# Fused RWKV-5 and tanh-shrink kernel: first four w_in pieces on SyncE's queue, own terms of units one to three as TensorE products, and another written order

## The chip, the core and the metric

One core of a Trainium2 chip runs the whole program. The metric is the device time of one execution in microseconds. Three runs of the kernel before took 582.51, 583.96 and 585.50 us; their median is 583.96 us. All times below are of that chip, in microseconds from the start of the profiled span unless said otherwise.

## What is computed

The first block is an RWKV-5 recurrence for 4 batches, 8 heads, 768 steps and heads of 48. The second is a dense layer with h - tanh(h) between two products. The output of the first, laid out as 3072 tokens of 384, is the input of the second.

```python
for t in range(S):
    kt, vt, rt = (k[:, :, t], v[:, :, t], r[:, :, t])
    cur = np.einsum('bhd,bhe->bhde', u[None] * kt, vt)
    y[:, :, t] = np.einsum('bhd,bhde->bhe', rt, state + cur)
    state = w[None, :, :, None] * state + np.einsum('bhd,bhe->bhde', kt, vt)
...
h = x @ w_in                 # 3072 x 384 by 384 x 2048
g = h - np.tanh(h)
out = g @ w_out              # 3072 x 2048 by 2048 x 384
```

The term of step t with itself, r_t * u * k_t summed over the head's 48 numbers, is what the kernel calls the own term. The two weight matrices come as float64 and are turned into float32 on the chip.

## The kernel before, in words

**Units.** The recurrence is cut into 24 units of 64 steps and two batches. A unit loads r, k and v in two halves each (96 KB a half, 192 bytes a packet), turns r and k over on TensorE into PSUM (L654, L806, L808), scales them by powers of w on VectorE and ScalarE (`scale_r`, `scale_k`, `copy_k`), and makes the 64 x 64 score matrices of its heads (`levels`, L730, all small products recorded at L606). VectorE copies what lies before the diagonal into the tile `at` (L830). The diagonal is the own term. `outputs` (L741) then multiplies `at` with v, `to_xt` and `to_rest` (L774, L779, ScalarE, recorded at L765) carry the result into the dense layer's input `xt`, and `to_state` and `keep` (L755, L789) go on with the state.

**Own terms.** A unit below `OWN` makes them as a product: ScalarE scales the turned k by w*u in four instructions (`own_k`, L706 to L709), TensorE makes 16 small products (`own_levels`, L711; each is two records in the trace), and VectorE copies the diagonal in one instruction (L821). A unit from `OWN` on does three VectorE instructions (r*k, times u, a sum over the head; L694, L824, L698) and eight small ScalarE instructions (`diagonal`, L702). `OWN` is 1, so unit 0 alone makes products.

**Dense layer.** Tile (j, f) is 256 tokens by 256 of the 2048 columns: 12 tiles j, of two units each, by 8 steps of f, 96 in all. It is: `h` in two halves of six TensorE records (L217), five ScalarE instructions (Arctan, Tanh, Tanh, Square, Relu: s, th, tg, sq, small), three on VectorE (g, m, cp; L242 to L246), and the product with w_out, either plain (`o`, L254) or with seven products for eight (`products`, L307), for which GpSimd adds parts of g (L290 to L294). PSUM holds two h tiles: `h` of the next tile but one waits for g of this one.

**Weights.** w_in and w_out come in 16 pieces (`Weights`, L134 to L191). A w_in piece is four loads: two main ones of 288 KB and two rests of 96 KB. The main ones go through SyncE's queue, the rests through GpSimd's (L589). A piece is then converted in seven steps on VectorE and ScalarE (L185 to L191). The pieces of w_in are numbers 0, 1, 4, 5, 8, 9, 12 and 13, the others are w_out.

**Loads.** All loads of a unit from unit 2 on are issued by SyncE; of units 0 and 1 ScalarE's queue issues the second halves (L647). From the second unit pair on, a part of the dense layer's input is moved across partitions by six loads per pair from GpSimd's queue, from the tile `rest` to `xt` (L786).

**Order.** `lay_out` (L540) makes 2400 tasks with an engine each. `Plan.written` (L364) emits them in the order of the string `ORDER`: each two characters are a task's number. Each engine executes its own instructions in that order and waits for what each needs. Numbers past the tasks are fill products on TensorE with the identity, whose result nobody reads (`fills`, L532, recorded at L534), and the place where the flag of w's range is read. The costs and data figures given to `add` take no part in what is emitted.

Of the kernel before, what the change touches and what calls it, by code (L numbers as in the profile page):

```python
# [42 lines left out]

DIGITS = "0123456789ABCDEFGHIJKLMNOPQRSTUVWXYZabcdefghijklmnopqrstuvwxyz+_"
ORDER = (
    "00010J2f2g2h2i2j2k2l2m2n0HbWbX02030K040605bWbWbW2o2q3534363231332r2t0I2s07370A0FbWbX080B0C2u2x2y38392v092w3U0D3C"
    "3B3V3W2p3A3G0U2z0L3R0M2+3S3T3D2_0N3F3H0V3Y0O3I0T3u3E3J0PbWbX3L3K3b0QbX3c300S3M3v3w3a0R3r3e3N3s3t3d0w3O3f3P3X3Z3g"
    "8D3Q3h3i3k0W0G3_4O3j0X8E0d430Y4P4Q3l4L0Z44404M4N453m8F0a3y463+0b3n413o0c423p3x3z15470ebYbYbY484p0u0E4Z8I4o4q0f8P"
    "4a0g494l0h4b4S4A4V4c0i4U4R4T4B3q4W0j8Q4m4n4C4X5I4v4Y4J5J5K4D8H4F0k4dbZ4e4K0l4I8L8R5F4G4f8G4H5G5H4z8SbZ4w134s8K8J"
    "4g5i8T8M8U4u4E4h8N4+8W4i4x8O8X8V4r4t4_8d4y4j5f505T0m525j5k510n5g5h5U8e0o8Y5L5V0p8p535M5N5W0q6C548g5P6D6E5X0r5O0t"  # L50
    "550s5Q698q5R5m565t6A6B8Z4k5S5A578h5lba5n595u8f5D5Y5p8i5B5v8j5C8a5Z5E5w6d8k8l5q6c6e8c5x5a6Z8m6N8b5o5b0v8n5r6a6b58"
    "145c6J8o6F5s5d6G6H8s6O775y8t6P6Q915z8r5e746R6n5+6o8u8w6I5_6j6K926L7678606p6g8x9D6M6373758v61666q688y6S6f6h676r64"
    "7W8z656T7X7Y9562946U937U98967T7V7H6i6V1D7I6k9E7J970xJ+996W9RJ_K06l6m796X7K0yJx9S6Y9H9F6s9I9J8+JyJz6t9T7A7B7h9G8_"
    "6u9K7L7D9A7C6vKP7EKM9d7F7G7a7i6w129e7j7Z7b906z6x7k9L6_KLKN9B6+7d9VKOKQ726y9WK9707M7l719C9X7N0z9M7cKA9U7O9f9YKu0+"
    "9Z7eKvKw7P9a9rKr7fK29i0_9N7Q1L7g7R9OKsKt9j16K1K3KZ9P177m9Q109h9g9b7n1811197o9l9k9s7p1ELF1F1TKBA17qKRL3LGLH9tKa7t"
    "9c1G7vKb7y9m9v7wA29w1A7u1H7x9z9n9xK61B9uLI9o9pLl9yA41CA5AFA3A81e1hKC1MLJLK1fAG1N9q1WKSKTA6KW1U1VAR1OA91g9+1PASAH"
    "1QAI9_A7L4AUAAA0AKAJAVANABKcAM1RALAfKD1SAgAT1I1xADLmLnAWAOACLoAYAjLpLqAZAiArAh7SAmAkAsAXL5AEAaB31iAv1jAtMAAP1J1k"
    "AnAwB41KAlAuAz1pAQAxAyM9MBB6AoBFA+B7LT1lBGBAB51mBTBH1nBIBJAb1XB81YMfB91oAcMgMh1ZBM2G2H1aBBBU2FBCBKBfAeBNBV1bBYBg"
    "Ad1cBXBWApBiBaBL1dAqBh1qBk2324KxA_1r26Bb251sKyKzBOB01t2E1yB1BjBt1z1u1+BuBm1_1vBZC3B2Bv1wByBDBcBw2P20BxC4BlB+BzBn"
    "BE27C5B_BP28Bo2921CH2AC82BBQC9C0C7CIC6BSBRCBBdCJCACM22BeCLCK2XCNCOCTKd2CBp2D2QBqCP2RCUBs2SCC2TChLzL+N4CWBrCXCiN3"  # L60
    "N52UCVCY2IC1CZCaCj2VCtCm2WCkC2CQCbClCDCnCpCoCE2JCq2KCuCF2LCGCcCRCw2MCvCyD52NCz2OCxD62YCS2ZD8C+D92aCdDCD7CeDACf2b"
    "DBDKCg2cDL7rC_DZD0DMDNDDDODa2dDP2eCrDbDRDcDe89CsDQDEDSD1DdDFDgDGDoDT85DUDp86DHEEDqDVDrDsEFDtDvDf87D2Du88EH81ETD3"
    "LUEUDhD4EGDwDIDiEVDxEJDjDJEIEKELDXDkEX8ADlEYEiEWDyEZEaDWEj8BDz8CD+ExEMEyENEbEmDYElEcE+82EkDmEpEOEn83E_FNEqEzF0Eo"
    "FOF3LVErDnFP84FQD_F2FSEd7sE1EeFRE0E2F1E3EPE4ERFTEQE5E6E7ESFVFUFcF4FdF5EsEgFgEtFeEfFfEhFhFjFrFiE8FWE9FsEBEAFkFXFl"
    "EvFuECFt7zFYFwG4FvEDFyFZG5F6FzEuEwG8F7FxGWFmG6F+G9FnF8G7GAGBFAGCF9FBFCGXF_FDGDG0GlGZFEFFFoGYFGGbFaFKGa7+Fb7_FHFp"
    "GeGE80GmFMGdFLFqGFGnFIGpG+GGGoG1GqFJGcG_GfG2GtH2GgGsH1GrG3H5GhH0GiGHGJH3GKGIGLH4GMHDGNGOGQHEGPGTH6HfK5HFH7HGGuGj"
    "HHGvHIHgHKGwHLH8HuHhK4GxHiH9HJHvGVHjGSHMHkHAGkHmHlK8HxI7HNHwKVHnHzHOGyH+HPHyGzHBK7HCI0KUH_KEHoI8HpHqKYIMHrIAGUI9"
    "KFGRLPICINI1IDIBI2HQIOIEI3IPI4KXIQIoIRIFIpK+IGIUKGIsHSISHTHRITIqL6IVJ1IHHUL7HVK_HsHWHXKHHYJ2KIHtIrKJJ5IvItKeHcIu"
    "IwHeJ4JGL1HdJ3IWJ6I5J8IIJ7LuIXHZIYJHKfHaIxHbKgL2JKIJJJJIJVJ9KhLOL0KKI6L_JLLWJWJNJAKiIKJOJMKnKjLXKpLQILLvIyJPJXIZ"
    "IzJZJYKoJaL8JBIbJbIcJCIaIdI+IeJcKlI_LMIfJQMCIgKqMDMEIhJ0JDIlKmIiJEJRJdInKkJFIkL9ImMjPJMNIjMiMkLRJSPKLSLAPNMOPMMJ"  # L70
    "JeJTPLPQPOJfPPMtPYJgLBPRJhPZMPLCPSLwPnNZPTPaLDMIPdPUPbPoPVPcPfLYPqPrJUPpPuPeJiN6PsNaNbPtPvQ0JkLLLNPgPwQ1PhLxPiQF"
    "Q2Q3LZMoQ4QGJlLyLaQHQ7Q5MuQIJjLEQKJmLbJnPWMKMpJoJpLcQUJqQJLkQ6QVLiQMPjJuPxPXLdQXJrM0JvLsM2QNPkNzMQQ8N7N8JsQjM1Lj"
    "Q9LrLtPyQLPlPzQWQAQOMRPmLgM3QYP+QPQZQbQaJwMvMFM4MLQQMGMHLfQkQRN+N_M5MMQBQyQCQlLeQmLhQcQoQzMmQpQdMlMnM6P_NcQnMwQD"
    "QqQeMqQ+JtRMM7R1QfM8Q_QgQrMxMSQsR2QEMsR0RNQtR3NjQSQuROQvRPRRRbRQRSRTQTR4RcR5MrR6QhReRfRUNiRdRqRVRgRiRhQiMTNHRrRW"
    "NIRXQwRjRtNdNeRYRuNARsQxR7RxN9NBRvR8RkS3NCRwRlS4RmSIS5S8SJS6O0S9NDS7R9SLSARBRCRARDREMURFRGRHRZNJMVRLNgNESBOURaMW"
    "NfNhNKRoMeMXO1O2RyMcMZRzSKSXRnSMR+SNMySPSOR_SQS0RpSROWSYSCOXOYOTOVSSSmSaSDSbSZSnMdSeScMaNnMbMzS_SoRKOrMYSdSTOsOt"
    "T0SpRISqSESrSFStS1SsSuT2SvS2NoSfSGSgTPT3ShT1T6SiT4TQOBSjNFSUTeTRT7TSO6NLSHTTM+SwTUSxTXTfM_SyTWSVT5TVT8TtTYTiN0Np"
    "OhSWThTuTlT9NkSkN1TxOvTgOuOwTjSlTvSzNqTZTwRJU6TAT+TBNGTaU7TbTmO7S+U9TkNMTyTnTzTCT_U8UATETDUDO4TFU0ULNmU1UMToTGOd"
    "THUaTIUNTMUPTpUOUbUBTqUSUQN2TcUdNNUCOCO3O5UpURUTTJUqTKUUTOODU2NOP3U3NlTNTdNPUETrOcNQUFOETsUGUcUHU4UeNYUfNTUhNrU5"
    "UINRNXOZNSUrUVNsOiUsUtUWV2O9UgUXOFNVUJUiNUO+UuUjUKNtUkUwV3NWOAUYV5UxUvO_UZV6UyV4V9NuUzP4U+OjUnNvU_TLVSUlOkOaObUm"  # L80
    "V7VTV8VAOlVBVhVUVCVXViOxVDVYVEOyOzUoVjVWV0VVVlVZVmV1VaVnVbVwVkVpVoVxVqVFO8V+VrVzVHVsW1NwVGVcVIVyNxW9VdV_NyVeW0VJ"
    "W2OGVKVLVfVMVNOHVgOeW3OIP5W4WAP0W5OfVtVuW6WBWEVQVvWDVOP6W7WCWFWGW8OJWHWOWIOgWJWPWMWSOKWdWQOOOLP7OROMOSOmWROPOQWe"
    "OnWKONWVWLP2OoWhVPWgWsWfP1OpWtWkWTWUWWX5WiWuWlX6OqWXWwWYWNWvWZWxWbWaX8W+WjWzP8WyWmXVX9WnP9W_PAXCX0WoXWPBX1X2WpWc"
    "X7VRXAWqXBXDXZXEWrXXXaXFXkXbXdXGXYX3XHXcXeXlXfXzXnPCX4XmPEXpPFXIXqPDPGXoX+XgXKXrXsXJX_XLY0YCY1Y2Y4YDY3XtXMXuXNXi"
    "YEXOXvY5YHXSYRYGPHYFYKXwYIYJYSXRYLPIYgY6YTXPYWY7YUXQYhXhXTXUXjYiYjXxYVYMYlYYY8YXXyYZY9YmYvYNYkYOYnYwYoYaZ8YpYzYb"
    "YyZ9YxZ0YcY+YdYAZAZDY_YBZBYPZCZEZGZYZ1Z2YQZFZHZZZ3ZnZ4ZcZ5ZaZbYeZdZfZeZgYfZhZoZIYqa0ZpYrZqZJZrYtYsZsZuZtZvYuZwa1"
    "ZiZKaFa4a2a3aGa5a8Z6aIa7aJaHZ7aKZLa6aMZxZNZjaLZOZMZkZPa9ZyaUZQZRZSZVaVaNaAaOZlaXaWZTaYZWZmaZZXabajaaacaPakaBaCZz"
    "ayalZUaoaQZ+apaRamanZ_araDaqadaEaeaSafagazbIa+b0b1bJa_b4b2b3aTbLb5bKahasbNatbMaib6bOaub7bPawbQavaxb8bRb9bBbCbAbD"
    "bEbSbFbGbHbUbTbV"
# [1190 lines left out]
```

## Time and profile before

| what | before |
|---|---|
| median of 3 runs | 583.96 us (582.51 to 585.50) |
| profiled execution, its own time | 582.57 us |
| its span in the profile | 580.8 us, so 1.8 us lie outside it |
| granted TensorE clock | 1.00 of full speed in nearly all slices |
| TensorE busy | 562.5 us (97%) |
| VectorE, ScalarE, GpSimd busy | 429.9, 404.3, 199.9 us |
| fill products on TensorE | 30 records at L534 |

The chain of waits that ended last runs over TensorE for 87% of the span. TensorE's records overlap one another, so its busy time includes the fill products and is no measure of useful work.

### The profile page before, as it was taken

Reading aid. Unit: us, or ns where it says so; the run is one execution under the profiler, and the core shown is the slowest. Engines: PE = TensorE matmul, PEld = TensorE weight load, DVE = VectorE, ACT = ScalarE, POOL = GpSimd, SP = SyncE. Lnnn points to the kernel's source line nnn. Section 1 sums busy time; section 2 is a strip of 40 time slices with the busy share of each in tenths; the row PEclk is TensorE's granted clock in tenths of the full one; section 3 lists DMA queues with packets and bytes.
Section 4 is the critical chain, followed back from the end, with each engine's and each line's share of the span. In section 5 each row is a group of like instructions: output and inputs, shape, how many; then the busy total and the mean of one; then the engine's idle time right before and its main releaser. Section 6 shows DMA issues by size and latency. Waiting matters only on the chain.

```text
span 580.8 us, 14137 instructions
## 1 busy us (share of the span) xinstructions
PE 562.5 (97%) x5487; PEld 480.4 (83%) x5487; DVE 429.9 (74%) x720; ACT 404.3 (70%) x926; POOL 199.9 (34%) x366
## 2 busy tenths in 40 slices
PE   7699999999999999999999999999999999999995
PEld 4467777777776789999888889989999988999994
DVE  4899878999998787967699796567676766454534
ACT  2699999999977566545884787577577568765550
POOL 5201111300000233546256184273455253463430
PEclk9999999999999999999999999999999999999999
DMA  8987857594620000132344451441233000010001
GB/s 137 171 199 145 140 117 118 120 173 109 142 64 5 1 1 1 28 56 44 54 67 85 61 105 23 68 89 17 45 63 61 2 21 16 5 30 2 19 11 32
DMA packets 138549, 38.48 MB, mean 66 GB/s; under 512 B 130761, under 2 KB 132905, under 8 KB 138473
## 3 DMA queue, kind: packets, MB, share of 16 engines
q1 hardware_dynamic: 130140, 29.71, 28.7%
q0 software_dynamic: 4992, 6.99, 5.3%
q10 hardware_dynamic: 3340, 0.79, 0.9%
q8 instruction: 45, 0.74, 0.5%
q14 instruction: 32, 0.25, 0.2%
...
## 4 chain that ended last, share of the span: by engine, by line
PE 87%; DMA 4%; ACT 3%; DVE 2%; issue 1%; SPq 1%; POOL 0%; ACTq 0%; DVEq 0%; POOLq 0%
PE h L217 41%; PE p L307 26%; PE o L254 10%; PE yk_ps L606 6%; DMA rt<-in_r_dram 2%; PE x_ps L656 1%; DMA vt<-in_v_dram 1%; DMA xt<-rest 1%; ACT at L704 1%; PE x_ps L606 1%; SPq L644 1%; ACT xt L765 0%; PE p L254 0%; PE x_ps L534 0%; POOL xt L786 0%
## 5 line engine op out<-in xcount | busy, mean ns | idle before, releaser
L217 PE MATMUL h<-xt,w_in_sb 128*128 128x256 f32 x1152 | 267.3, 381 | 0.2 <-DMA xt<-rest 0.2
L217 PEld LDWEIGHTS h<-xt,w_in_sb 128*128 128x128 f32 x1152 | 214.9, 190 | 32.5 <-DVE g L242 1.5
L290 POOL TENSOR_TENSOR sg<-g 128x256 f32<-128x256 f32 x69 | 55.1, 800 | 197.7 <-DVE g L246 130.1
L242 DVE TENSOR_TENSOR g<-h,th 128x512 f32<-128x512 f32 x96 | 65.8, 686 | 67.9 <-ACT tg L233 25.2
L229 ACT ACTIVATE s<-h 128x512 f32<-128x512 f32 x96 | 57.1, 594 | 54.3 <-PE h L217 47.2
L307 PE MATMUL p<-mixed,sg 128*128 128x192 f32 x426 | 92.3, 327 | 0.0
L244 DVE TENSOR_TENSOR tg<-s,tg 128x512 f32<-128x512 f32 x96 | 69.3, 724 | 29.2 <-ACT s L224 19.4
L233 ACT ACTIVATE tg<-h 128x512 f32<-128x512 f32 x96 | 56.9, 594 | 41.9 <-PE h L217 29.9
L246 DVE COPY_PREDICATED g<-small,tg 128x512 f32<-128x512 int32 x96 | 72.0, 761 | 12.0 <-ACT small L235 9.0
L231 ACT ACTIVATE th<-h 128x512 f32<-128x512 f32 x96 | 56.7, 593 | 32.7 <-PE h L217 32.6
L307 PEld LDWEIGHTS p<-mixed,sg 128*128 128x128 f32 x426 | 73.3, 190 | 1.3 <-issue 0.3
L307 PE MATMUL p<-w_out_sb,g 128*128 128x192 f32 x284 | 70.4, 330 | 0.3 <-DVE o L335 0.3
L235 ACT ACTIVATE small<-s,smallb 128x512 f32<-128x512 f32 x96 | 68.5, 721 | 1.2
L254 PE MATMUL o<-w_out_sb,g 128*128 128x384 f32 x192 | 67.3, 489 | 0.0
L786 POOL DMA_DIRECT2D xt<-rest x66 | 32.5, 496 | 91.7 <-ACT rest L765 91.1
L224 ACT ACTIVATE s<-s 128x512 f32<-128x512 f32 x96 | 60.7, 633 | 1.4
L307 PEld LDWEIGHTS p<-w_out_sb,g 128*128 128x128 f32 x284 | 50.6, 190 | 3.1 <-DVE o L335 0.6
L254 PEld LDWEIGHTS o<-w_out_sb,g 128*128 128x128 f32 x192 | 35.8, 190 | 19.4 <-DVE parts L267 0.2
L704 ACT ACTIVATE at<-same,du 128x64 f32<-128x64 f32 x184 | 48.2, 342 | 0.5 <-DVE du L700 0.4
L292 POOL TENSOR_TENSOR sg<-sg,g 128x128 f32<-128x128 f32 x69 | 39.1, 569 | 3.1
L294 POOL TENSOR_TENSOR sg<-sg,g 128x128 f32<-128x128 f32 x69 | 37.2, 542 | 3.4
L307 PE MATMUL p<-mixed,g 128*128 128x192 f32 x142 | 34.7, 326 | 0.0
...
## 6 DMA issues: line engine op xcount, KB each, us to landing
...
```

The source lines that it names most:

```text
L217: self.nc.tensor.matmul(t.h2[:, z], self.w_in_sb[:, t.f // 2, kk, z * 128 : (z + 1) * 128], self.xts[t.j][:, kk].rearrange("p b t -> p (b ...
L224: A.activation(t.s, t.s, AF.Square, scale=G3)
L229: A.activation(out, t.h, AF.Arctan, scale=G2)
L231: A.activation(out, t.h, AF.Tanh)
L233: A.activation(out, t.h, AF.Tanh, scale=G1)
L235: A.activation(out, t.s, AF.Relu, bias=self.smallb, scale=-1.0)
L242: V.tensor_tensor(t.g, t.h, t.th, ALU.subtract)
L244: V.tensor_tensor(t.tg, t.s, t.tg, ALU.mult)
L246: V.copy_predicated(t.g, t.small.bitcast(I32), t.tg)
L254: self.nc.tensor.matmul(self.outs[i], t.g2[:, z, i * C : (i + 1) * C], self.w_out_sb[:, t.f + z, :], start=t.first and z == 0, stop=t.last ...
L290: add(t.s4[:, :2], g[:, 0::3], g[:, 1:2].to_broadcast([128, 2, C]), ALU.add)
L307: self.nc.tensor.matmul(ps[bank][:, half * n : (half + 1) * n], a, b, start=t.first and half == 0, stop=t.last, skip_group_check=True)
```

## The change

Three edits. `OWN` goes from 1 to 4. For pieces below number 6 (0, 1, 4 and 5, the first four of w_in) the two rests are issued by SyncE and not by GpSimd. The string `ORDER` is another one, for the tasks that these edits leave (2394), with 9 fill products where there were 15.

```diff
-OWN = 1
+OWN = 4
...
 ORDER = (
-    "00010J2f2g2h2i2j2k2l2m2n0HbWbX02030K040605bWbWbW2o2q3534363231332r2t0I2s07370A0FbWbX080B0C2u2x2y38392v092w3U0D3C"
...
+    "00012i2j2k2f2g2h2l2m2n0I0HbQbR02030K042q35060J0A2o320C34360531332s0B2r2ubQbQ2x072v2y2t370838392w0U092z0L0M3S3C2p"
...
-            queues, data = (("SP",), (3.0,)) if n % 4 > 1 else (("SP", "POOL") * 2, (1.2, .95) * 2)
+            queues, data = (("SP",), (3.0,)) if n % 4 > 1 else (("SP", "SP" if n < 6 else "POOL") * 2, (1.2, .96 if n < 6 else .95) * 2)
```

The two strings, read with the tasks' numbers, say this of the first stretch. `u3` is unit 3, `W1` weight piece 1, `W1.c0` to `W1.c6` the steps of its conversion, `rest` and `main` a piece's loads, (0,0) a dense tile, Ha and Hb the halves of its h, Oa and Ob those of its product with w_out.

```
loads by SyncE and ScalarE, to r of unit 2
  before: w, u, main W0, unit 0 (six halves), main W0, unit 1 (five), u again as bonus, k of 2, main W1, last v of 1, r of 2
          (GpSimd: both rests of W0; then, beside the loads of 2 to 4, rests of W1, W4, W5)
  after:  w, u, unit 0 (six halves), rest main rest main of W0 among the loads of unit 1, main W1, k of 2, half r of 2, main W1, r of 2
          (then: rest W1, k and r of 3 with the last rest of W1 between, the bonus, k of 4, one rest of W4, r of 4)
ScalarE from unit 1's state to rest of unit 3
  before: keep u1, diagonal u2, table load and warm-up, diagonal u2, W1.c2 W1.c3, s(0,0), diagonal u3, xt and rest of u2, copy k3,
          diagonal u3, sq(0,0), W2.c2 W2.c3, diagonal u4, xt and rest of u3
  after:  keep u1, own_k u2, W1.c2 W1.c3, tg th s(0,0), xt and rest of u2, copy k3, own_k u3, sq(0,0), diagonal u4 (both halves),
          small(0,0), xt and rest of u3         (table load and warm-up stand ahead of xt of u1)
TensorE from the turning of unit 5 on
  before: turned 5 | Oa Ob(0,0) Ha(1,0) levels 5 ...
  after:  turned 5 | Ha Hb(1,0) Oa(0,0) levels 5 ...
```

## Rows read from the trace of the kernel before

**Rows 1.** The page: busy time by engine.

```profile
PE 562.5 (97%) x5487; PEld 480.4 (83%) x5487; DVE 429.9 (74%) x720; ACT 404.3 (70%) x926; POOL 199.9 (34%) x366
```

**Rows 2.** Windows: busy us of each engine, TensorE's clock, DMA share, GB/s.

```profile
20.00:25.00 5.00, 2.73 (x74) 1.87 (x74) 3.64 (x6) 2.41 (x8) 1.01 (x2) 1.00 1.21 174
...
35.00:40.00 5.00, 5.00 (x131) 3.32 (x132) 4.91 (x11) 4.94 (x15) 0.00 (x0) 1.00 0.76 143
...
46.00:575.00 529.00, 526.06 (x4809) 455.37 (x4807) 395.25 (x658) 374.64 (x844) 185.80 (x320) 1.00 0.30 57
...
75.00:85.00 10.00, 8.82 (x163) 6.91 (x165) 7.24 (x13) 9.11 (x30) 1.72 (x4) 1.00 0.60 150
```

**Rows 3.** The chain of waits: start, us, what.

```profile
15.20 7.33 DMA rt<-in_r_dram
...
22.66 0.63 PE x_ps L656 x4
...
25.44 1.49 PE h L217 x6
...
59.15 1.29 PE o L254 x4
```

**Rows 4.** TensorE in the timeline: start, us, engine, line, operation.

```profile
12.63 0.97 PE L606 MATMUL x_ps<-rT,kU 48*64 48x64 f32 x32 [1.01 <-ACT kU L709]
...
33.89 2.74 PE L534 MATMUL x_ps<-ident 128*128 128x512 f32 x6
...
50.41 1.46 PE L217 MATMUL h<-xt,w_in_sb 128*128 128x256 f32 x6
```

**Rows 5.** ScalarE in the timeline.

```profile
12.23 0.97 ACT L709 ACTIVATE kU<-kT,w_u 128x128 f32<-128x128 f32 x3
...
25.51 1.04 ACT L795 ACTIVATE state<-yk_ps,power 128x96 f32<-128x96 f32 x4 [0.80 <-PE yk_ps L606]
26.42 1.07 ACT L704 ACTIVATE at<-same,du 128x64 f32<-128x64 f32 x4
27.51 1.28 ACT L572 ACT_TABLE_LOAD   x1
...
37.70 0.93 ACT L187 ACTIVATE power<-power,p_bias 128x768 uint32<-128x768 uint32 x1
...
41.72 0.92 ACT L765 ACTIVATE rest<-yk_ps 64x64 f32<-64x64 f32 x4
...
43.15 0.60 ACT L233 ACTIVATE tg<-h 128x512 f32<-128x512 f32 x1
```

**Rows 6.** VectorE: three rows of the timeline, one group by form.

```profile
13.66 0.75 DVE L821 COPY_PREDICATED at<-same,x_ps 128x512 f32<-128x512 int32 x1 [1.19 <-PE x_ps L606]
...
15.70 0.56 DVE L185 TENSOR_SCALAR power<-st 128x768 uint32<-128x768 uint32 x1
...
21.70 0.94 DVE L191 TENSOR_TENSOR w_in_sb<-w_in_sb,power 128x768 f32<-128x768 f32 x1
...
L700 DVE TENSOR_REDUCE du<-rk 128x8 f32<-128x384 f32 x23 | 12.5, 544 | 0.2
```

**Rows 7.** Loads: timeline; issues from 42 on (last: us to landing); SyncE's waits.

```profile
8.30 0.60 SPq L644 DMA_DIRECT2D first_k<-in_k_dram  x1
...
17.85 1.64 POOL L171 DMA_DIRECT2D st<-in_moe_w_in_dram  x3
...
42.69 2.91 POOL L786 DMA_DIRECT2D xt<-rest  x6 [19.94 <-ACT rest L765]
...
xt<-rest POOLq DMA_DIRECT2D x6, 16.0 KB, 3.8
...
SPq L644 <- DMA first_k<-in_k_dram: 3.1, 1, 3.1
```

**Rows 8.** One h that follows closely on g, in the timeline; such waits in all.

```profile
388.83 2.46 PEld L217 LDWEIGHTS h<-xt,w_in_sb 128*128 128x128 f32 x12 [0.20 <-DVE g L242]
...
PEld h L217 <- DVE g L242: 1.5, 7, 0.3
```

More of the change, by code (lines that the diff above doesn't have):

```diff
@@ L45 @@
 ORDER = (
-    "00010J2f2g2h2i2j2k2l2m2n0HbWbX02030K040605bWbWbW2o2q3534363231332r2t0I2s07370A0FbWbX080B0C2u2x2y38392v092w3U0D3C"
[L47 to L89, printed above, removed]
+    "00012i2j2k2f2g2h2l2m2n0I0HbQbR02030K042q35060J0A2o320C34360531332s0B2r2ubQbQ2x072v2y2t370838392w0U092z0L0M3S3C2p"
@@ new lines @@
+    "2+3T3U0N3A3B2_3Q3E0O0D0S3D3F3P3R3G0PbR3J3K303V3H3Z0T0G3I3a3q0Q0V3L3r3s0R3M3W3X3Y3N3o3c3b873O3n3p0W3d0F3g0X4I3x0Y"
+    "4J4K0E3e3h0w0Z883f4F0a4G4H3i8B0b8A3u893w4P3t3v3j3y0c0d4j3z3kbT8J4T4f3+3l3_4U424M4V4g4h8C40434W414X8EbT444i4k8F8D"
+    "4L4N0e4O453m4Q0l8K0f8G464R4S5D4E478L4A4l4t0gbT4Y4B4m4n4u490h4v5A4D4Z4C4w4pbT4a0i8M595B4o4b0j5C5E4q5F8X0k8N4c5G5H"
+    "488Y8Q4x5Z0m5a5b8H4s4d4r8b5d8O0n5c5e4y5N8P5f5J0o5O8j0t4z0p638R8Z5K0q665I8c4+5P67688d0r64655M8k8a5n4_0s5g5h8I8S50"
+    "6W5L8T5Q6X6Y4e5651586T5R6H535S5o6U6V578V5p556A8n8U5T548m146I5q696B8e5U155j5r8q705k5V6h5i0v8f8x6z525W8g8y5m6D6abU"
@@ new lines @@
+    "8W5X6+6_8l6J8h71725l6K6i5s8z0u8o978p5t6L6j8r6E8+7Q7B5u908s7R7S5Y6C6Z6b5v8i136F7O0x6G7C8t7N7P5w128_5z5x8u73916293"
+    "74756k607D5_1D0y6M610z5+988w6N6l925y6O8v7b9B6d9A6c7T946P6eJu9L6fJs99776Q1L1695JrJt176g6R7U7V9C969EJvJw7E6S7c6m9D"
+    "7d0+9F9M7F6n0_769N9G789P6oKI109QKJKK7A9X116pJy79JxJz1U9Y9O7X6q9T9S9HKp7e6v6rKF6x7f6y7GKGKH1W9Z6w1T9c9IKoKq7H6u9a"
+    "6t9R7Y9J9U7I9b1E9K6s7W7JKM1F9VK0Kl9e7KKLKN9W7ZKmKn7a7L9dK31V7g9f18LD7M9l197hKT1G1A7i1H9g9m1I7j1B9h7k1J9p7r9i1C9o"
+    "7p9n7o9s9q1e7n9x1M1g9r7q9tL97s9k9y1NLCLE9j1h9u1O1f1K9v9_9+1X1p1P9wLALBA29z1QA9A01Y1R1ZAA1S1aALA3A11xACKrA4AMAD1b"
@@ new lines @@
+    "ABA51cANAOAGLgAPA61dAEAFAHAZ2524A723AI26AQKsKt1iA8AaLfLh1jAS1kAJK41lATAK1qAb1rARAlAeAUAdAcAmAfAg1sAhAz1mAnAo1nA+"
+    "AqApAiAV1oA_B0AsB22E2HAW1y2GAX2F1t1zB9K5B1AtArB4BAAY1uB31+BNAu1v1_AjBC1wBD20BO2PB5AkBQB6BB27BPAvBGBEBRBHBZBF21BS"
+    "AwBUBT28BI29BaBV2A7lBnAyK62BBoK7Ax22BcB72CBd2XBb2DBqB8BeBgBfBJBhBpBWBsBK2QBrKQBtBvLiBzBuLjLkBwB+Bi2RCBC02IBM2S2J"
+    "CC2TBLC1BX2UB_C22VBY2KC52L2WBjCD2MCGBkC4CEC3BlCNCHBm2NCFBxC62OBy2Y2ZC7CJ2aCICO2bCK2cCbCQCRCPCcCUCSC9CVC8CfCTCnCe"
+    "CACdCWCgCL2dChCiCoCj2eCMCp83Cs7_CXCqCkCr80CY84CZCvC_8586D0CuCaDED1D3CtDFD4CwD2ClD5D6DGD7DTDI7xDHKzDUDLM4D8M3M5Di"
@@ new lines @@
+    "DWD9DJDADjDKDMDVDNCmDk81DY7yDn82CxDODXDmDaDPCyDlDbDBDZCzE8DQDpC+E9KUKVDcDCEBDqEADd7zECDDEDDeDoDR7tDfKWLNDSEE7mMZ"
+    "DrENMaMbEFDsLOEODtEGDuDg7+EQEPK+KXEcK_7uEREHDhES7vETEIDvEUEVDxEJDwEWEKDyEdDzEXD+D_EYELEeE0EZEhE1E2EMEfE5EiE3LPEa"
+    "E7Eg7wE6EkE4EbEjElErEmEsEnEoFHEtEvEuFIEwExEzEpFLEyFJE+EqFMFKE_FPFWFNF0FOFXF1FQFlFRFYFaFSFZF2FTFbFdF4FcFeF3FfFmF5"
+    "FgF6F7FUFhFoF8FiF9FpFnFAFVFBFqFsFDF+FrLtFCLuMzF_FtM+M_FuGQFEG2FvG1G0GRFFG5G3FwFGG4G6FjFxGUG7GTFkGSGXG8GVG9FyGWGY"
+    "GAGZFzGaGBGbGDGcGEGCGFGGGdGHGKGIGfGLGJGMGNGgJ_GOGPGuGiGjGhGeGmGkGvGlGnKOGoH7GwGpGxGzH8GqGyGrG+G_GsHAH0H9K2HBHZKP"
@@ new lines @@
+    "HCHEHDGtH1HaHFH2HGHoH3HbHdKvHHHcH5HeH4HgHIHfHhH6HJHiHpHjJ+HKHkHrHlHqHMHLHsHNHtHOHvI1HuHwHPI2HxHQHyHTIGI5HzI3HRHV"
+    "I6IHHSHUHWI7I9HYHmIKK1H+IIHXILHnI4KuIOIMK8I8IJIAIiINIBK9IjICKRIDKAImIPLIIkKSIQIxIlKBIRIpIyISKwInKCIqJAI+KDIzLFKE"
+    "KYI_LJJ0J2IoJBKZJ1IrKaKxJDJCJPKbJ3LGLHKyJQJFLoKcJ4H_JGKjKdJELKKkKeJSKiI0JIJRKfKhIEJUJHIsL0LpJJKgIFJVItL1IuL2J5JT"
+    "LvJ6LQITJXJ7L3IVLRIUIWLmJWM7PDJYJKM6M8IXIYLlLnIvJLIZIaJMIcPEIbIeLLMdIdIwPHMcMeIfPFPSMCLMPGJZPIIgJ8PJPLIhJaPKJ9Jb"
+    "PMMHJNPNMIMDPOJOMnPPMJJcMoJeJfJdJgJhPQJiNTJjNUNVJlL4JkJnJoJmPRL5LqMAJqN1JpPTL6M9MBNuPhL7PWL8PUPVPiN0N2PXPZNtNvPa"
@@ new lines @@
+    "LSPlPkPjPwPoPYPmPbPxLwPpPcLTQ9PzLrPdPyPeP+PfPnQ1MiP_PqQAQ0Q2PrQOQ3QDPsQCQBQPQGQ4QENBPtQHQdOOQSQ5QRONOPQQQeQ6QVLx"
+    "QsQTMpQgQWQFQtQUQIQfQXLUQhQvPgMKMEMfMgMhPuLVQkQJNWLsQKNXNYPvLWQLQuQ7LXMjLbQwLYQYMLQzLyNCLeQiQZQjQlQ8LcQxMGQaQMQy"
+    "LaLdQmLZN7QNQ+QnMFQbQoLzQcQpNhRGQ_N6NiR0RHNDR1L+R2RIRLRJQqMkRMRKN4QrL_RONxR3RNNwNyM0RPN3N5RVR5MqRQR6OlR7RRR8OmOn"
+    "RWMrM1RSM2NjRkRZO5RYRXRlRcRaO6RdRzRoRnRmR+RrRpRsSCS0RbSDR_ReS2RfMMSFRgS1RhRqR4S4SES5SRS3R9SHRDS6RCSSRtRASIRuRTMl"
+    "STRvSURwSGRBRUNcRFSVSKRiRESWSJS7SXSLRjS8SYSgS9MNSMSZShSNSaSORxMmSiMORyMPNZNdSASjMQSvNEMWMRMYMSSBSlMTN8SmSbSPSkMX"
@@ new lines @@
+    "NaNbSnScOQSQSoSdOROSSeSpSqSwMVSrSfObMUSxSsOcNFStSzO7SySuS+T0TJS_T1T2TKT3TYT4TNT5TMTLTZTQTOTPTRTnTbTSTaToTcTTTdTU"
+    "TeTgT6TVTrTfTpThT7T8TsT9TiTtTAMsTvTqTjTBTWMtTkTCTuTFMuTDTGTwU0TEMvN+TxNANzN_THU1MwTyO1TIMxUFTzU4MyU3N9U2TXU5TlU6"
+    "U8NkU7O0NGU9NlUATmNgUBUGUCOdNfUUUJOXUHNHUIUVUKUMULUNNIUWUOUjNJO2UPNeOUT+O8UQOpURUZOTOVT_UXOWUaUDUYNKUbUEUcO9NSNL"
+    "USNRUdNQNONMUTNPOoOqNNNmUeUfUhNnUgO3NoOzOuO4UiNpUkOYNqO+UyO_UnNrUmNsUlUzUqOsOeOrOtVMU_OvV0U+VNV3UoUpUrVbVPUsVOVc"
+    "VQUtV1UuV2V4OAUvVRV5VSUwVUVfV6OBVdUxVeOaV7VgV8OCVhVjVTV9P0VVVBViVAODVWVCVkVqVXOEVDOZP1OMVrOIVEVlVFVZVsVGOKVvVmVH"
@@ new lines @@
+    "OFW3VwVYOGVLVuVnVtW4VyOLOfVxOJVIVaVzW7VKW5OwWIV+W8W9WBVJWJW6V_OHWAW0OgWCWKWMWDVoWNWOWEWQWFWLVpWPW1WROxWSW2WTWGOy"
+    "WUWHOhWVWWWXWYWmWbWZWaWnWcWfOiWpWeWqW_WdWtWoWgOjX0WhWiWkX3WjWrXPWsWuX2WvOkWlX6WwX1WzX4WxX5WyX7P2X8XQX9P3XAXeXBXS"
+    "XTXRXfXWXUXVXXXtXiXYXhP4XgXZXlXjXaXkXmW+XbP5XnXCXoP6XDXEP8XFPBXuXGPCXHXIXpY6XJXMXwXKXqXxXNXvY7X+P9XyXOX_XcXLY8PA"
+    "Y9P7XzXdYBY0YLYCY1YAYMY2YEY3YDXrYOYFYPYNYaYSYGYQYHYRYTYbYIYUYpYdYeYcYqYhYfYgYiZ2YtYjYrZ3YsYuYvYxXsZ5Z6Y4YwYVZ4Z7"
+    "YyYWY5Z8ZAYXYJZ9YkZBZSYlYmYKZTYzY+ZhZUY_ZVZXYYZYZWYZZaYnZZZCZbZDYoZEZ0ZcZdZiZeZ1ZkZlZFZjZoZmZGZnZpZHZqZwZIZrZJZx"
@@ L90 @@
+    "ZKZsZLZMZOZfZNZzZPZyZRZ_ZQZga0ZtZuZ+a1a2a9a3aAa4a5aOaCa6aBaEaPaFZvaRaQa7aDaTaHaSa8aGaUaIadaVaJaWaeaKaXaLasagahaY"
+    "afatakaZaiaaajalbCawamavaMauanazaxaobDa+apaNbGbFabbEbJbHacaybKbIa_aqb0b1bLarb2b3b5b6b4b7b8bMb9bAbBbObNbP"
 )
```

## The prediction

> **What bounds the kernel now.** First the busy times of the page: TensorE is busy 562.5 of 580.8 us, VectorE and ScalarE far less [rows 1]. The windows then say where TensorE is not full. From 46 to 575 us it is busy 526.1 of 529.0 us, and 1.2 of the 2.9 us that it lacks lie between 75 and 85 [rows 2]. So what the change saves on other engines after 46 us is worth nothing by itself, and the time that can go lies ahead of the first product that has nothing but full TensorE behind it: H(1,0), which starts at 50.41 [rows 4]. What holds that product back is read in three views. In the chain of waits the load of unit 2's r lands at 15.20 + 7.33 = 22.53, and h(0,0) starts at 25.44 [rows 3]. From there ScalarE works without a gap to speak of, 4.94 of 5 us between 35 and 40 [rows 2], up to the end of `rest` of unit 3 at 41.72 + 0.92 = 42.64 [rows 5]; TensorE meanwhile makes fill products, one group of them 2.74 us long [rows 4]. GpSimd then issues the six moves from `rest` to `xt` from 42.69 on, 2.91 us for all, each 3.8 us under way [rows 7]: the last lands at about 48.9, 6.2 us after `rest` was done. The chain to be followed is thus load, ScalarE, moves; after it TensorE.
>
> **The yardstick.** The profiled execution took 582.57 us, 1.4 less than the median of 583.96. The differences below are worked out on the former and subtracted from both. About 0.5%, 2.9 us, is what a measurement of this kernel can tell from no change: faster means under 581.0, slower over 586.9.
>
> **Step a, the loads up to unit 2's r.** The rests of W0 move to SyncE's queue, main and rest stand behind unit 0, and the bonus leaves its place ahead of r. SyncE gains eight issues of about 0.60 and GpSimd loses as many of 1.64/3 = 0.55 [rows 7]; half of them stand behind r of unit 2 in either order. SyncE's queue once stood still for 3.1 us until an earlier load had landed [rows 7]. At best the new order fills that time less one issue: r lands at 22.53 - 3.1 + 0.6 = 20.0. At worst it lands as now, 22.5, since 20 to 25 is a stretch with the data engines full (share 1.21, 174 GB/s) [rows 2]. Ahead of r there are 96 KB more than before, 0.55 us at that rate, so I take 20.0 + 0.55 = 20.55. Turning it takes 0.63 [rows 3], and one group of small products is left before h(0,0), which I take at 0.6 (the like group with kU took 0.97 [rows 4]). h(0,0) starts at **21.8, 3.6 sooner**; ends 21.2 and 25.4. Its weights must be there too: converting W0 took from 15.70 to 21.70 + 0.94 [rows 6], and with W0 landing some 2 us sooner it ends at about 20.6, so r is late, not W0. If r came sooner yet, W0's conversion would be next.
>
> By the Trainium skill, page "DMA: Bandwidth & Descriptors", section "Issuing engines are not separate DMA queues", loads of all engines end on the same 16 data engines, and issuing from several saves only the issue time. The share of 1.21 in the trace agrees that they are shared. By this rule alone the move to one queue gains nothing and adds 8 x 0.60 = 4.8 us of issues to SyncE; rival B below has its time.
>
> **Step b, ScalarE from h(0,0) to `rest` of unit 3.** Now 25.51 to 42.64, 17.1 us. Table load, 1.28, goes ahead of the stretch; four half groups of `diagonal` at 1.07 go (4.28); one pair of W2's conversion at 0.93 each goes behind it (1.86). Added are two `own_k` of four instructions, 0.97 x 4/3 = 1.3 each (2.6), a second half group of unit 4's `diagonal` (1.07), th and tg of (0,0) at 0.60 each (1.2) and one more instruction of that size, small (0.6) [rows 5]. Sum: -7.42 + 5.47 = -1.95, so 15.2 us: `rest` ends at 21.9 + 15.2 = **37.1 instead of 42.64**. Nothing on VectorE holds this up: a unit with own products saves three instructions of 0.55 and adds one of 0.75 there [rows 6], 2.7 us for three units.
>
> **Step c, the moves.** GpSimd has none of the rests ahead of them any more. The 6.2 us stay: the last lands at 43.3, and H(1,0) starts then, **7.1 sooner** than 50.41.
>
> **Step d, what moves behind it.** Oa and Ob(0,0) stood ahead of H(1,0) and now follow it, 2 x 1.29 [rows 3]: 2.6 of the 7.1 are only an exchange. That leaves 4.5. The own products are new work for TensorE, 3 x 0.97 = 2.9 at most [rows 4]; they all stand ahead of H(1,0), where TensorE idles or makes fills, and cost nothing while ScalarE is the bound there. If that cover went, they would cost 2.9.
>
> **Step e, the order in the full stretch.** An h tile needs the PSUM of the last but one, so Ha must not come too soon after g. In the old order one h follows with only two halves of o between it and the h that it waits for, and it waited 0.20; all such waits come to 1.5 us, the longest 0.3 [rows 8]. In the new order there are ten such places. The price is not shown for all; below, nothing, if each finds its g done; above, one VectorE instruction ahead of g each time, 0.20 + 0.94 [rows 6, 8]. I take the measured 0.20 for nine more: **1.8 lost**. Other work that moves in the full stretch I cost at nothing: TensorE covers it.
>
> **Sum.** 4.5 - 1.8 = 2.7 gained. The profiled execution would take 579.9, the median **581.3**.
>
> **Rivals.**
> D, nothing is lost in the middle: the ten places are covered, and the 1.2 us between 75 and 85 [rows 2], which fall into one hole of TensorE, go too, as other work now stands there. For it: the waits of this kind are short and few. Against: ten places for one. 4.5 + 1.2 = 5.7, so 578.3.
> B, the loads come no sooner: the head of SyncE's queue still waits for landings, with more behind it, and r of unit 2 lands at 22.5. For it: the share of 1.21. Against: the 3.1 us in which the queue stood still. Then the 3.6 are lost and 4.5 - 3.6 - 1.8 = -0.9: 584.9, no change to a measurement. This is also the case in which moving rests between queues doesn't do what it says.
> C, slower: the close h tiles wait for a late g, as VectorE or ScalarE is busy with a conversion or a diagonal when h ends. At 0.20 + 0.94 for ten places, less the 0.2 of now, 11.2 are lost and 4.5 gained: 590.7. It decides from (4.5 + 2.9)/10 = 0.74 per place. For it: ScalarE is busy 9.11 of 10 us between 75 and 85 [rows 2]. Against: no such wait is over 0.3 now.
>
> **Chances.** Forecast 0.46, D 0.22, B 0.20, C 0.12. The forecast lies 0.3 above the bound of faster, so its 0.46 falls half to either side: faster 0.22 + 0.23 = 0.45, same 0.23 + 0.20 = 0.43, slower 0.12. The range reaches from D with another 0.9 (r at 20.0 and a little of the 15.2 us) to B with 0.7 more for the ten places: 577.4 to 585.6. It leaves out nearly all of C and the rest of D's lower end.
>
> **What would show it.** In the changed profile: r of unit 2 landing near 20.5 and h(0,0) at 21.8 (a); `rest` of unit 3 ending near 37.1 with ScalarE full before it (b); six moves landing near 43.3 and H(1,0) right behind (c); fewer fills and TensorE full from there on; ten or so waits of h for g of about 0.2 (e), with C if they are 0.7. What comes late next could be the loads of units 4 to 6, needed some 7 us sooner through a queue with more in it: a row of TensorE waiting for r, k or v after 43 would say so and make the forecast wrong, as would h(0,0) at 25 (B).

## The result and the profile after

Over 20 runs the changed kernel took 584.53 us in the median (582.49 to 587.95), and 20 runs of the kernel before 581.56 (580.63 to 591.42). The ratio is 1.0047, with a 95% interval of 1.0029 to 1.0064: slower by about 0.5%, where 0.5% faster was forecast. The three runs known at the time of the forecast had a median 2.4 us above that of the 20, so the forecast's 2.7 us gained stand against 3.0 us lost.

The profiled execution of the changed kernel had a span of 586.1 us and took 587.95 us, 3.4 above the median and the longest of the 20, so its holes need not be those of the median. The page, to be read beside [rows 1]: every engine but TensorE is busy for less time, as the own terms had it, and TensorE for 2.5 us more.

```profile
PE 565.0 (96%) x5571; PEld 482.8 (82%) x5571; DVE 427.8 (73%) x714; ACT 403.0 (69%) x914; POOL 198.0 (34%) x358
...
PEclk9799998999999999999999999999999999999998
```

The second row is the granted clock of TensorE in 40 slices, in tenths: it is down in the second slice and the seventh, where before it was full. Next the windows (busy us of TensorE, its weight loads, VectorE, ScalarE, GpSimd, then clock, DMA share, GB/s):

```profile
20.00:26.00 6.00, 5.39 (x99) 4.31 (x92) 3.71 (x6) 1.95 (x6) 0.00 (x0) 0.50 0.86 105
...
84.00:88.00 4.00, 1.47 (x11) 1.21 (x10) 3.80 (x8) 3.89 (x14) 0.00 (x0) 1.00 0.59 124
88.00:92.00 4.00, 4.00 (x10) 2.44 (x10) 2.07 (x4) 3.12 (x10) 0.00 (x0) 0.57 1.00 284
```

From 20 to 26 us TensorE works at the lower of its two levels (0.50 is 1.2 GHz). From 84 to 88 it stands still for 2.5 us, and then works at 0.57 for four more, which by that figure (4 x 0.43, an estimate) costs another 1.7. In the timeline of TensorE four of the h products that are the first to need a new `xt` now wait; before, H(1,0) started without a wait [rows 4], and one later h waited for 0.23 us:

```profile
49.16 1.18 PE L216 MATMUL h<-xt,w_in_sb 128*128 128x256 f32 x4 [1.70 <-DMA xt<-rest]
...
67.42 2.83 PE L216 MATMUL h<-xt,w_in_sb 128*128 128x256 f32 x12 [0.79 <-DMA xt<-rest]
...
87.32 2.07 PE L216 MATMUL h<-xt,w_in_sb 128*128 128x256 f32 x6 [2.53 <-issue]
...
124.25 1.10 PE L216 MATMUL h<-xt,w_in_sb 128*128 128x256 f32 x4 [0.64 <-DMA xt<-rest]
```

They are h(1,0), h(2,0), h(3,0) and h(5,0): 5.7 us in all. The third is put down to "issue", a wait for nothing that the profile shows. But its moves show what it is. In GpSimd's rows for the tile `xt`, the last two moves of unit 7 are issued at 80.8 and 81.3 and land 5.9 us later, at 87.2 the second, 0.1 us ahead of the product; before, all six of that unit were issued from 73.8 to 76.2 and took about 5.0:

```profile
L785 POOL DMA_DIRECT2D xt<-rest x2: 487/487/487, 80.8 to 81.3; - x2
...
DMA to landing us min/median/max: 5.9/5.9/5.9
```

So the last stretch that waits for the recurrence is not over at h(1,0), as the forecast had it. It lasts to h(5,0).

### The profile page after: what moved, and what is told of

Its sections match the earlier page's. It is cut to its first block, busy times and chain, and to the rows that moved or that the text cites. A ratio compares the mean times of both kernels' runs of the same rounds, so it can differ in the third digit from the quotient of the medians.

```text
span 586.1 us, 14342 instructions
## 1 busy us (share of the span) xinstructions
PE 565.0 (96%) x5571; PEld 482.8 (82%) x5571; DVE 427.8 (73%) x714; ACT 403.0 (69%) x914; POOL 198.0 (34%) x358
## 4 chain that ended last, share of the span: by engine, by line
PE 85%; DMA 5%; ACT 4%; DVE 2%; issue 1%; POOL 1%; SPq 1%; ACTq 0%; POOLq 0%; DVEq 0%
PE h L216 41%; PE p L306 28%; PE o L253 8%; PE yk_ps L605 6%; DMA xt<-rest 3%; POOL xt L785 1%; DMA vt<-in_v_dram 1%; DMA kt<-in_k_dram 1%; ACT xt L764 1%; PE x_ps L655 1%; ACT rest L764 1%; PE x_ps L605 1%; SPq L643 0%; PE p L253 0%; ACT power L186 0%
## 5 line engine op out<-in xcount | busy, mean ns | idle before, releaser
L289 POOL TENSOR_TENSOR sg<-g 128x256 f32<-128x256 f32 x69 | 53.7, 779 | 213.1 <-DVE g L245 185.6
L245 DVE COPY_PREDICATED g<-small,tg 128x512 f32<-128x512 int32 x96 | 73.3, 767 | 10.6 <-ACT small L234 6.4
L703 ACT ACTIVATE at<-same,du 128x64 f32<-128x64 f32 x160 | 41.6, 339 | 0.4 <-DVE du L699 0.2
L291 POOL TENSOR_TENSOR sg<-sg,g 128x128 f32<-128x128 f32 x69 | 40.1, 582 | 4.7
L293 POOL TENSOR_TENSOR sg<-sg,g 128x128 f32<-128x128 f32 x69 | 38.1, 553 | 4.5
L306 PE MATMUL p<-w_out_sb,sg 128*128 128x192 f32 x142 | 34.7, 327 | 0.0
```

The lines of the kernel that those rows point to most:

```text
L245: V.copy_predicated(t.g, t.small.bitcast(I32), t.tg)
L289: add(t.s4[:, :2], g[:, 0::3], g[:, 1:2].to_broadcast([128, 2, C]), ALU.add)
L306: self.nc.tensor.matmul(ps[bank][:, half * n : (half + 1) * n], a, b, start=t.first and half == 0, stop=t.last, skip_group_check=True)
```

## The experiments

Times are ratios to the kernel before, measured in the same rounds on the same chip. Different experiments stem from different rounds and chips, so two ratios are told apart only where their intervals lie apart.

### Which stretch holds the loss

The two orders were cut at the first half of h(1,0) and put together crosswise. Tasks that one kernel does ahead of the cut and the other behind it stand right at the cut.

```diff
early_after:   changed order up to Ha(1,0)
-              changed order behind it
+              order before behind it
early_before:  order, own terms and queues before up to Ha(1,0)
-              order before behind it
+              changed order behind it
```

> The new order up to h(1,0), the old order from there (own terms as products and rests on SyncE's queue as in the change). Theory E, the loss arises ahead of h(1,0): 1.005 of before, as the whole change (584.5 on the scale of the 20 runs, where before is 581.6). Theory L, it arises behind h(1,0), in the order of the full stretch: 1.000 or less (581.6 or below). If each has its part as the two traces have it (1.3 us ahead, some 2 us behind): 1.002.

> The old order, own terms and queues up to h(1,0), the new order from there. Theory E: 1.000. Theory L: 1.005. Each its part: 1.003. By theory L the trace has waits of TensorE between 60 and 125 us for the moves into xt and for g, about 2 us in all, as that of the change has.

The new order up to h(1,0) gave 0.9998 (0.9974 to 1.0023), the new order behind it 1.0069 (1.0042 to 1.0096). Theory L holds: ahead of h(1,0) nothing is lost or won, to within some 1.4 us either way, and the loss lies behind it, 4.0 us by the second kernel (2.4 to 5.6). In that kernel h(3,0) has the same hole, and the low clock behind it (0.63):

```profile
86.50 1.90 PE L217 MATMUL h<-xt,w_in_sb 128*128 128x256 f32 x6 [2.02 <-issue]
```
```profile
88.00:92.00 4.00, 4.00 (x9) 2.12 (x8) 1.76 (x4) 2.79 (x8) 0.00 (x0) 0.63 1.00 276
```

### The hole at h(3,0)

In the new order o(2,0) stands behind the first half of h(3,0); at h(4,0) the o of the tile before stands ahead of the h, and there is no wait there. The experiment exchanges the neighbours.

```diff
 TensorE: unit 8's outputs, unit 9 turned
-Ha(3,0)
 Oa(2,0) Ob(2,0)
+Ha(3,0)
 levels 9, Hb(3,0)
```

> The change with one exchange of neighbours on TensorE: the product o(2,0), two halves that stand right behind the first half of h(3,0), stands ahead of it. Theory M, that h waits for the six moves into xt of unit 7 (2.5 us idle in the trace of the change, and about 1.6 us more at a granted clock of 0.50 behind it): the two halves fill the wait, the clock stays at 1.00, and the time is 2 to 4 us below the change's, 0.998 to 1.001 of before. Rival I, the 2.5 us are a stall of TensorE's own instruction stream that recurs wherever it stands: 1.005, the hole stands elsewhere. Rival O, o(2,0) isn't ready there, as its g is late: the hole stays ahead of o(2,0).

It gave 1.0002 (0.9978 to 1.0025), so 0.45% less than the change, about 2.6 us. The timeline and the window of this kernel:

```profile
85.00 2.82 PE L253 MATMUL o<-w_out_sb,g 128*128 128x384 f32 x8
87.66 1.46 PE L216 MATMUL h<-xt,w_in_sb 128*128 128x256 f32 x6
```
```profile
88.00:92.00 4.00, 4.00 (x81) 3.32 (x80) 3.97 (x8) 3.65 (x12) 0.00 (x0) 1.00 1.01 275
```

o runs where the hole was, h starts without a wait, and the clock stays at 1.00. The hole doesn't turn up at another place, which speaks against a stall of the instruction stream. So do two other kernels, further down, that keep the change's order there: in `after_more_fills` and `after_pool_rests` the last move lands at about 85.1 and 88.4, and h(3,0) starts 0.1 us behind it, at 85.18 and 88.49, with 2.1 and 2.4 us of idle time before it. One exchange of neighbours thus takes back all of the loss that can be measured.

Doing the same at h(2,0) and h(1,0) too:

```diff
 TensorE: unit 5 turned
-Ha(1,0) Hb(1,0) Oa(0,0)
+Oa(0,0) Ha(1,0) Hb(1,0)
...
-Ha(2,0) Hb(2,0) flag Oa(1,0)
+flag Oa(1,0) Ha(2,0) Hb(2,0)
```

> The same exchange at three places: o(2,0) ahead of h(3,0), the first half of o(1,0) ahead of h(2,0), the first half of o(0,0) ahead of h(1,0). Theory M: besides the 2 to 4 us of the run above, up to 0.8 at h(2,0) and 1.3 of the 1.7 us at h(1,0) are filled: 0.995 to 0.999 of before. Rival I: 1.005.

It gave 1.0046 (1.0021 to 1.0070): worse than the one exchange in the same rounds, 586.2 against 583.1 us. The expectation took any o for ready:

```profile
48.70 1.53 PE L253 MATMUL o<-w_out_sb,g 128*128 128x384 f32 x4 [1.08 <-DVE w_out_sb L190]
...
68.73 1.90 PE L253 MATMUL o<-w_out_sb,g 128*128 128x384 f32 x4 [1.77 <-ACT rest L764]
```

o(0,0) now waits for W2's conversion, which the change had moved behind, and o(1,0) for ScalarE, 1.1 and 1.8 us, where h(1,0) and h(2,0) had waited 1.7 and 0.8. The filler must be work that is ready.

### Fills and the clock

```diff
 TensorE: w and u turned
+fill fill
 unit 0 turned, ... levels 1
+fill
 own products 1
+fill
 unit 2 turned
```

> The change with four more fill products: two behind the turning of w and u, one (of two) ahead of unit 1's own products, one ahead of the turning of unit 2's k. Theory C, the granted clock of 0.50 between 20 and 26 us comes from TensorE's idle time ahead of it and delays all that follows: the clock stays at 1.00, h(0,0) starts some 1.0 us sooner and the time is 1.0 to 3.0 us below the change's, 1.000 to 1.003 of before. Rival, the stretch is bound by loads and by ScalarE, so the clock costs nothing: 1.005, with the clock at 1.00.

1.0052 (1.0028 to 1.0076), the rival's figure: no gain, though the profiled execution shows what was wanted, a clock of 1.00 and h(1,0) at 47.43 instead of 49.16. The gain is waited away behind it:

```profile
0.00:25.00 25.00, 21.33 (x343) 13.23 (x343) 15.06 (x29) 11.93 (x29) 6.84 (x33) 1.00 0.90 144
```
```profile
47.43 0.96 PE L216 MATMUL h<-xt,w_in_sb 128*128 128x256 f32 x3 [1.76 <-DMA xt<-rest]
...
85.18 1.39 PE L216 MATMUL h<-xt,w_in_sb 128*128 128x256 f32 x4 [2.13 <-issue]
```

The fills were put on the exchange as well:

> The exchange at h(3,0) and the four more fill products, both on the change. If what is gained ahead of h(1,0) counts once the hole at h(3,0) is shut (the fills alone brought h(1,0) from 49.16 to 47.42 in the trace): 1.5 us below the exchange alone, 0.997 of before. If the moves into xt set the pace as before and fill the gain with waits at h(1,0) and h(2,0): 1.000, with longer waits there.

1.0009 (0.9984 to 1.0034), the same as the exchange alone. And in this execution the clock was low with the same fills in place:

```profile
0.00:25.00 25.00, 20.88 (x253) 12.67 (x253) 14.29 (x27) 9.62 (x21) 6.82 (x33) 0.81 1.00 146
```

So the fills alone do not decide the clock of the first 25 us. It was 0.80 to 0.93 in the five profiles with the new order's start, `OWN` at 4 and no fills added, 1.00, 0.81, 1.00 and 0.83 in the four with them, and 1.00 in the four profiles of the kernel before and of it with the rests or the own terms alone changed; `early_before`, whose start is exactly that of the kernel before, had 0.95. So it differs between executions of the same start; whether the order has a part in it as well, one profile of each kernel doesn't show.

### The loads

The rests alone, on the kernel before, and their undoing in the change:

```diff
-queues = ("SP", "POOL") * 2
+queues = ("SP", "SP" if n < 6 else "POOL") * 2
```

> The kernel before with the rests on SyncE's queue at their old places and nothing else changed. If the queue holds loads up: k and r of unit 2 land later, by up to four issues of 0.6 us and a wait for an earlier landing, 1.003 to 1.008. If the data engines alone set the landing: 1.000.

> The kernel before with the rests on SyncE's queue once more, as the first run gave 0.9981 with an interval that holds 1. If the queue alone is worth 0.2%: 0.9975 to 0.9985. If the first run was chance: 0.9995 to 1.002.

> The change with the rests of the first four w_in pieces back on GpSimd's queue, at the places where the new order has them. If SyncE's queue holds the loads up (r of unit 2 landed at 23.35 in the change, 22.53 before): h(0,0) some 1 us sooner, 1.002 to 1.004 of before. If the order behind h(1,0) is all of the loss: 1.005 or more, as the rests then stand in GpSimd's queue ahead of moves into xt.

On the kernel before, SyncE's queue gave 0.9981 (0.9956 to 1.0005) and again 0.9978 (0.9954 to 1.0001). Each interval just holds 1; the two agree, and the second fell where 0.2% had been expected. Taken together the two intervals give about 0.9962 to 0.9997 (an estimate): the queue alone is probably worth some 0.2%. Taking the rests back from the changed order gave 1.0031 (1.0006 to 1.0057), an interval that overlaps the change's. The queue is at any rate not the loss. By the Trainium skill ("DMA: Bandwidth & Descriptors", "Issuing engines are not separate DMA queues"), issuing from several engines saves the issue time only. The runs agree so far as the eight more issues on SyncE, 4.8 us, are not seen in the time.

Then r of unit 2 itself, on the exchange with the fills:

```diff
 SyncE: v of 1
-main W1, k of 2, half r of 2, main W1, half r of 2
+k of 2, half r of 2, half r of 2, main W1, main W1
```

> As the run above, and the two main loads of W1 (288 KB each), which stand among the loads of unit 2, moved behind r of unit 2 on SyncE's queue. By step a of the forecast r then lands at 20.5 to 21.5 and not at 23.35, h(0,0) starts at 21.7 to 22.5, and the time falls by up to another 1.5 us: 0.994 to 0.997. Rival: the conversion of W0 on VectorE ends no sooner than 22 us, so h(0,0) moves by 1 us at most and the next weights come later: 0.997 to 1.000.

1.0004 (0.9979 to 1.0029): the gain that was expected is missed, and the rival is nearer. SyncE issues r from 14.05 on and it lands 3.4 us later, at about 18.4, five microseconds sooner than in the change; h(0,0) starts at 23.55. Rows of the timeline (SyncE, then TensorE) with the landing of `rt` between:

```profile
14.05 1.87 SPq L643 DMA_DIRECT2D rt<-in_r_dram  x2
```
```profile
DMA to landing us min/median/max: 3.3/3.4/3.5
```
```profile
23.55 1.56 PE L216 MATMUL h<-xt,w_in_sb 128*128 128x256 f32 x6
```

With the fills on the change alone, where W1's main loads still stood among those of unit 2, r was there by 22.1 at the latest and h(0,0) started at 23.53, at a clock of 1.00 too. So r's landing does not set it as long as r is there by 22.2, when TensorE comes to turn it. Later it does: in the kernel with `OWN` at 2 further down, TensorE waits for r and h(0,0) starts at 25.00, also at a clock of 1.00. Rows of TensorE in `after_more_fills`, then in `o20_own2`:

```profile
22.24 0.65 PE L655 MATMUL x_ps<-ident,rt 128*128 128x128 f32 x4
...
23.53 1.56 PE L216 MATMUL h<-xt,w_in_sb 128*128 128x256 f32 x6
```
```profile
23.83 0.63 PE L655 MATMUL x_ps<-ident,rt 128*128 128x128 f32 x4 [0.66 <-DMA rt<-in_r_dram]
...
25.00 1.56 PE L216 MATMUL h<-xt,w_in_sb 128*128 128x256 f32 x6
```

What held TensorE until 22.2 with r at 18.4 is said by the chain of waits (start, us, what):

```profile
10.45 4.61 DMA first_k<-in_k_dram
...
17.03 1.28 ACT kU L708 x4
...
19.29 0.69 PE x_ps L605 x32
...
22.94 0.68 PE yk_ps L605 x32
```

k of unit 1, then `own_k` of unit 1, its own products, its outputs and its state: the new products of unit 1 stand in the chain to h(0,0). The chain holds an added fill of 1.06 us as well. That h(0,0) would come sooner without the products is not shown: in the kernel with `OWN` at 1 further down it started at 26.99. And it could not have come more than one microsecond sooner, since the conversion of W0, whose columns h(0,0) needs, ends at 22.60, as the rival had it:

```profile
21.64 0.96 DVE L190 TENSOR_TENSOR w_in_sb<-w_in_sb,power 128x768 f32<-128x768 f32 x1
```

### The own terms

On the kernel before, with nothing else changed:

```diff
-OWN = 1
+OWN = 4
 own_k of units 1 to 3 where the first half of the diagonal stood
 own products behind levels, their copy behind that of levels
```

> The kernel before with the own terms of units one to three as products, placed where the diagonals stood; loads and the rest of the order as before. By the forecast's step b ScalarE loses 1.7 us ahead of rest of unit 3 and the kernel gains up to that: 0.997. Rival, the products and the second copy on VectorE stand in the chain of each unit (0.75 and 0.97 each), and ScalarE does not bound: 1.002 to 1.004.

1.0031 (1.0010 to 1.0053): slower, the rival's side. ScalarE in the timeline of this kernel, to be read beside [rows 5]:

```profile
35.09 0.60 ACT L229 ACTIVATE s<-h 128x512 f32<-128x512 f32 x1 [3.77 <-PE h L217]
...
45.71 0.92 ACT L765 ACTIVATE rest<-yk_ps 64x64 f32<-64x64 f32 x4
```

ScalarE has less to do and stands still for it: 3.8 us ahead of s(0,0). `rest` of unit 3 ends at 46.63, 4.0 later than in [rows 5], though h(0,0) started at 25.83. Step b took ScalarE's busy time for the bound; here ScalarE waits for TensorE. TensorE stands still at nearly the same place in both kernels, before and here:

```profile
29.77 0.69 PE L606 MATMUL x_ps<-rT,kT 48*64 48x64 f32 x32 [2.21 <-issue]
```
```profile
30.35 0.69 PE L606 MATMUL yk_ps<-rT,state 48*64 48x64 f32 x32 [2.96 <-ACT warm L572]
```

The second wait is put down to the table load and its warm-up, which stand behind `own_k` of unit 2 in this order and end 0.67 us ahead of the product. The clock between 25 and 50 us was 0.93 here and 1.00 before. How much of the 4.0 us is the longer chain of the products, how much this wait and how much the clock was not taken apart.

The converse, on the exchange at h(3,0) in the new order:

```diff
-OWN = 4
+OWN = 1   (o20_own1; bonus ahead of k of 2 again)
+OWN = 2   (o20_own2; bonus right behind r of 2)
 r*k, times u and sum behind the scaling of r, both halves of the diagonal where own_k stood
```

> The change with the exchange at h(3,0) and OWN at 1 again: units one to three make their own terms on VectorE and ScalarE, the diagonals stand where own_k stood, the three VectorE steps behind the scaling of r, and the bonus is loaded ahead of unit 2 as before. If the products cost here what they cost in the old order (0.3% alone): 0.997 of before. If they save ScalarE's time, as step b of the forecast had it: 1.003 or more, with rest of unit 3 later.

> As the run above with OWN at 2: unit 1 keeps its products, units 2 and 3 lose them, and the bonus stands right behind r of unit 2. If the products cost by the second copy of units 2 and 3 on VectorE and their place in TensorE's chain: 0.997 to 0.999 of before. If they save: 1.002.

1.0075 (1.0047 to 1.0103) and 1.0030 (1.0007 to 1.0054): against the 1.0002 of the exchange alone the products of units 1 to 3 save 0.7%. For units 2 and 3 alone it would be 0.3%, but there the two intervals overlap. The bonus, which has to come sooner, is a part of both numbers that was not taken apart, and the diagonals stand in an order that wasn't written for them. So much is shown: an order that is written for one way of making the own terms of units 1 to 3 costs time when the other way is put into it.

### Early gain, old order behind

> The new order up to h(1,0) with the four more fills and W1's main loads behind r of unit 2, and the old order from there. The new order up to h(1,0) with the old one behind was 0.9998. If early time counts one for one in the old order: 0.995 to 0.998. If the first product o(0,0), which waited 1.1 us for W2's conversion in that run, and the moves hold the rest: 0.999 to 1.000.

The changed order up to h(1,0), with fills and the late W1, then the old order: 1.0015 (0.9992 to 1.0038). Nothing is gained, and what was expected if early time counts one for one is missed. In its profile the clock of the first 25 us was 0.83 and h(0,0) started at 28.73, so the early gain wasn't there in this execution; it also has o(0,0) waiting 1.1 us, as in the first of these hybrids:

```profile
51.33 2.82 PE L253 MATMUL o<-w_out_sb,g 128*128 128x384 f32 x8 [1.08 <-DVE w_out_sb L190]
```

No version was found that beats both kernels beyond its interval. The nearest is the kernel before with the rests on SyncE's queue.

## Why the prediction was wrong

Two terms of the sum failed. The 4.5 us that steps a to d gain ahead of h(1,0) measured nothing (0.9998), and the 1.8 us lost behind it measured 4.0 (1.0069), as step e put at nothing the other work that moves there. The time of 584.5 lies in the stated range and 0.4 from rival B by luck: the range was worked out from a median of three runs that lay 2.4 above that of the 20. Against the kernel before, the forecast was 2.7 gained, B 0.9 lost, and the runs show 3.0 lost.

**Step a** failed. r of unit 2 was to land at 20.55; its halves were issued at 14.8 and 16.1 and took 7.2 us, so the second landed at 23.3 (SyncE in the change, its waits, the landing of both halves, then TensorE):

```profile
16.13 0.60 SPq L643 DMA_DIRECT2D rt<-in_r_dram  x1
...
SPq L643 <- DMA vt<-in_v_dram: 2.5, 1, 2.5
...
DMA to landing us min/median/max: 7.2/7.2/7.2
```
```profile
23.49 1.09 PE L655 MATMUL x_ps<-ident,rt 128*128 128x128 f32 x4
...
25.54 2.13 PE L216 MATMUL h<-xt,w_in_sb 128*128 128x256 f32 x6
```

The step had the standing of SyncE's queue filled. But the queue stood still for 2.5 us all the same, both main loads of W1 were issued ahead of r's second half, and that half was issued at 16.13, 1.0 later than before, where the step had it 2.5 sooner. How much the 288 KB loads count for is not shown: with the same loads in front, r was there by 22.1 in `after_more_fills`. And the step is wrong at a second place: that nothing but r is late. With r at 18.4 h(0,0) started at 23.55, and the forecast had 21.8. Unit 1's own products, which step d costed at nothing, are on that chain, and W0's conversion ended at 22.60 and not at the forecast's 20.6. In the change h(0,0) started at 25.54. From r at 23.3, and the 1.2 us from its turning to h(0,0) in `o20_own2`, it would have started at about 24.6 at a clock of 1.00 (an estimate); the rest, about 0.9, is the low clock. With r on time and a clock of 1.00 the new order has it at 23.5, 1.9 sooner than before.

**Step b** failed in its reason. From state of unit 1 to `rest` of unit 3 it measured 25.68 to 42.25, 16.6 us, against 15.2 forecast and 17.1 before (ScalarE in the change):

```profile
25.68 1.04 ACT L794 ACTIVATE state<-yk_ps,power 128x96 f32<-128x96 f32 x4 [0.43 <-PE yk_ps L605]
...
30.76 0.60 ACT L232 ACTIVATE tg<-h 128x512 f32<-128x512 f32 x1 [1.27 <-PE h L216]
...
41.34 0.91 ACT L764 ACTIVATE rest<-yk_ps 64x64 f32<-64x64 f32 x4
```

The count of ScalarE's work held: it is busy for 14.4 us of that stretch, 16.5 before, 2.1 less where 1.95 were forecast. But ScalarE is no longer full there and stands still for 2.1 us, 1.27 of them for h(0,0), where before it was 0.6.

**Step c** was nearly right: 42.26 to 49.0, 6.8 us, against 6.2. H(1,0) started at 49.16: 1.25 sooner than before, not 7.1.

**Step d** was right on the exchange, 2.6 us. With it the change is 1.3 us behind at h(1,0) in the two profiles, and level with before by the first hybrid. That the own products cost nothing there did not hold in the order before, where the own terms alone cost 0.3%.

**Step e** was right in size and wrong in scope. All waits of h for g are these, against 1.5 us in [rows 8]:

```profile
PEld h L216 <- DVE g L241: 2.7, 10, 0.4
```

1.2 us more, where 1.8 were forecast. The sentence that failed is the one beside it, that other work that moves in the full stretch costs nothing since TensorE covers it. The new order has the moves of unit 7 five microseconds later, and no other task stands between the turning of unit 9 and h(3,0): 2.6 us by the exchange, close to the whole loss. That the price of the hole is more than its length, as the clock behind it is down, is seen in the profile only: the median clock of the runs is 0.992 in the change and 0.9925 with the exchange.

**Rivals.** B (loads no sooner, 584.9) came nearest in time and in what r did, but its reason is only a part: with r at 18.4 the kernel was no faster. C was on the right side with the wrong wait: it looked at h behind g and not at h behind the moves. What the forecast named as late next, loads of units 4 to 6, was not seen but for one wait of 0.2 us for an r; the moves were.
